# Attention over 16 blocks of heads: K of a block in one load, part of its tokens moved by GpSimd, scores in six pieces

## The chip, the cores and the metric

The kernel runs on one core of one Trainium2 chip. The metric is device time in microseconds (us) of one execution; a difference of about 0.2% is what a measurement of this kernel can tell from none. The engines are TensorE (PE; its weight loads are PEld), VectorE (DVE), ScalarE (ACT), GpSimd (POOL) and SyncE (SP). SP issues every DMA of this kernel, so all transfers run in one queue, in the order in which SP issues them.

## The reference

```python
B, H, Sq, Skv, Dh = 8, 16, 16, 2048, 256      # bfloat16
scores = jnp.einsum('bhqd,bhkd->bhqk', q, k) * Dh ** -0.5
attn = softmax(scores, axis=-1)
return jnp.einsum('bhqk,bhkd->bhqd', attn, v)
```

There are 128 heads, each with 16 queries and 2048 keys of 256 elements. K and V are 134 MB each and every byte of them is read once.

## The kernel before, in words

Eight heads make a block: their 8 x 16 queries are the 128 rows of a score tile. There are G = 16 blocks, numbered 0 to 15 (`last` is 15). A block's K is 8 MB and its V is 8 MB, 128 tokens on each of 128 partitions; below, K(j) and V(j) are those of block j.

**Buffers.** `SL` holds four slots of 64 tokens per partition (4 MB each): VA and VB together are the window of V (`VW`), KA and KB take the two halves of a block's K (half e = 0 or 1 is four heads, loaded in rows of 64 tokens, 32 KB). V comes in rows of 128 tokens, 64 KB. `QT` holds the transposed queries, `O_all` the output of all blocks, `PTz` the transposed probabilities spread over zeros, `QW` the queries of one block spread over zeros.

**Loops.** Each engine runs its own loop over blocks, and semaphores tie them together:

- DVE transposes K in place, 32 tokens at a time (`kt`, L198-200, counted by `c_kt`, and by `c_k0` for block 0), takes the row maximum of the scores (L222), transposes the probabilities twice (L226, L227) and copies a part of them into `PTz` (`copies`, L202).
- PE computes the scores of a block in four groups of 16 matmuls of 512 columns (`qk`, L302), counted by `c_qk`; then `SPARE` = 5 times four matmuls into `X_ps` that nothing reads; then 128 matmuls of probabilities by V (`pv`, L309-320, called PV below), counted by `c_pv` in eight steps a block.
- ACT spreads the next queries into `QW` (`qwb`), takes the exponential (L281-282), makes the rest of the copies (L269) and scales the output (`evac`).
- SP issues K in two halves as soon as the scores of that half of the block before are done (`c_qk`), and V as soon as PV of the block before is done (`c_pv`).
- GpSimd works at the start only: it clears buffers and makes 16 copies of the queries (L184), one behind the other, then clears the second half of `PTz` (L189). The last counts `c_pool` to 2.

**The start.** The queries land in `PTz`, DVE transposes them (L194), and GpSimd copies them from there to `QT`. K(0) is loaded into the slots of V, and K(1) into KA and KB at once behind it, without a wait (L135-137). DVE transposes K(0) as it lands, and then the first half of K(1); only behind that it waits for `c_pool` (L219) and enters its loop. V(0) follows when the scores of the first half of block 0 are done (L140).

**The end.** V of the last two blocks comes in smaller pieces (`PIECES`), and SP issues each when the tokens in its place have been used.

Of the kernel before, what the change touches and what calls it, by code (L numbers as in the profile page):

```python
# [10 lines left out]
SP = mybir.EngineType.SP  # L11
BF16 = mybir.dt.bfloat16
# [3 lines left out]
SPARE = 5  # L16
VA, VB, KA, KB = 0, 1, 2, 3
# [3 lines left out]
def bass_standalone__softmax_full_bidir__sampling_kernel(  # L21
# [16 lines left out]
    ku = k.rearrange("b h s d -> (b h s) d").rearrange("(u p t) d -> u p t d", p=128, t=T)  # L38
# [4 lines left out]
    with ExitStack() as es:  # L43
        ec = es.enter_context
        SL = ec(nc.sbuf_tensor("SL", [128, 4, T, D], BF16))
        QT = ec(nc.sbuf_tensor("QT", [128, SQ * D], BF16))
        QW = ec(nc.sbuf_tensor("QW", [128, 2, 128, 8], BF16))

# [8 lines left out]
        O_all = ec(nc.sbuf_tensor("O_all", [128, G + 2, D], BF16))  # L57
# [8 lines left out]
        def sem(name):  # L66
# [3 lines left out]
        s_k0 = [sem("s_k0a"), sem("s_k0b")]  # L70
        s_k = [sem("s_ka"), sem("s_kb")]
        s_kl = [sem("s_kla"), sem("s_klb")]
        s_v = sem("s_v")
        s_v0 = sem("s_v0")
# [5 lines left out]
        c_k0 = sem("c_k0")  # L80
        c_kt = [sem("c_kt0"), sem("c_kt1")]
# [10 lines left out]

        SLf = SL[:].bitcast(F32)

        QX = PTz[:, 1, 0:SQ * D // 128, :].rearrange("p t m -> p (t m)")

        QXu = QX.rearrange("p (c u a y) -> p a u c y", u=8, a=4, y=2)

        QTu = QT[:].rearrange("p (c u y) -> p u c y", u=32, y=2)

        SLk = SL[:].rearrange("p s (c t) (b i q) -> p s c b q t i", t=16, i=32, q=2)


        PIECES = {last - 1: [(0, 60), (60, 39), (99, 29)],
                  last: [(0, 28), (28, 32), (60, 23), (83, 16), (99, 11), (110, 8), (118, 5), (123, 5)]}

        s_p = {a: sem("s_p%d" % a) for a in sorted({a for w in PIECES for a, n in PIECES[w][1:]})}
        VW = SL[:, VA:VB + 1, :, :].rearrange("p a t d -> p (a t) d")

# [10 lines left out]
        def qx(Q, a):  # L120

            return (QTu[32 * a:32 * a + 32, 8 * Q:8 * Q + 8, :, :].rearrange("p u c y -> p c u y"),
                    QXu[32 * Q:32 * Q + 32, a, :, :, :].rearrange("p u c y -> p c u y"))

        def load_k(eng, g, e, slot, t0, n, s):
            eng.dma_start(SL[:, slot, t0:t0 + n, :], ku[2 * g + e, :, t0:t0 + n, :]).then_inc(s, 16)  # L126

        def on_sync(eng):
            def load_v(w, a, n):

                eng.wait_ge(c_pv, 8 * w + (a + n + C - 1) // C)
                eng.dma_start(VW[:, a:a + n, :], vb[w, :, a:a + n, :]).then_inc(s_p[a] if a else s_v, 16)  # L132

            eng.dma_start(QX, qh).then_inc(s_q, 16)
            for g, s0, s in ((0, VA, s_k0), (1, KA, s_k)):  # L135
                for e in range(2):
                    load_k(eng, g, e, s0 + e, 0, T, s[e])

            for e in range(2):
                eng.wait_ge(c_qk, 4 * e + 4)  # L140
                eng.dma_start(VW[:, T * e:T * e + T, :], vb[0, :, T * e:T * e + T, :]).then_inc(s_v0 if e else s_v, 16)
            for e in range(2):
                eng.wait_ge(c_qk, 4 * e + 12)
                load_k(eng, 2, e, KA + e, 0, T, s_k[e])
            for e in range(2):
                eng.wait_ge(c_pv, 4 * e + 12)
                eng.dma_start(VW[:, T * e:T * e + T, :], vb[1, :, T * e:T * e + T, :]).then_inc(s_v0 if e else s_v, 16)
            with nc.Fori(3, last, engines=[SP], hint_back_edge=True) as j:
                for e in range(2):
                    eng.wait_ge(c_qk, 8 * j + 4 * e - 4)  # L150
                    load_k(eng, j, e, KA + e, 0, T, s_k[e])
                load_v(j - 1, 0, 2 * T)
            for e in range(2):
                eng.wait_ge(c_qk, 8 * last + 4 * e - 4)
                load_k(eng, last, e, KA + e, 0, T // 2, s_k[e])
                load_k(eng, last, e, KA + e, T // 2, T // 2, s_kl[e])
            for w in PIECES:
                for a, n in PIECES[w]:
                    load_v(w, a, n)
            eng.wait_ge(c_ev, G)  # L160
            eng.dma_start(oh[:, 0:last, :], O_all[:, 2:G + 1, :]).then_inc(s_st, 16)
            eng.wait_ge(c_ev, G + 1)
            eng.dma_start(oh[:, last, :], O_all[:, G + 1, :]).then_inc(s_st, 16)
            eng.wait_ge(s_st, 32)

        def on_gpsimd(eng):

            for x, n in ([(c_pv, 8)] + [(x, 1) for x in s_kl] +
                         [(s_p[a], 16 * G - 16 * sum(a in dict(PIECES[w]) for w in PIECES)) for a in s_p]):
                eng.sem_inc(x, n)  # L170
            eng.memset(QW[:].rearrange("p e m x -> p (e m x)").bitcast(F32), 0.0).then_inc(c_qt, 1)
            zero = [PTz[:, e].rearrange("p t c -> p (t c)").bitcast(F32) for e in range(2)]
            eng.memset(zero[0], 0.0).then_inc(c_pool, 1)
            eng.memset(mk[:], 1.0).then_inc(c_mk, 1)
            eng.memset(P_sb[:, 0:16], 0.0).then_inc(c_mk, 1)
            eng.memset(P_sb[:, 2064:2080], 0.0).then_inc(c_mk, 1)
            eng.wait_ge(c_mk, 3)
# [3 lines left out]
            for n in range(16):  # L181

                eng.wait_ge(c_cq if n else c_pool, max(n, 1))
                eng.tensor_copy(*qx(n // 4, n % 4)).then_inc(c_cq, 1)  # L184

            eng.wait_ge(c_qw, 4)
            eng.wait_ge(c_cq, 16)
            eng.wait_ge(c_mk, 7)
            eng.memset(zero[1], 0.0).then_inc(c_pool, 1)  # L189

        def on_vector(eng):
# [6 lines left out]
            def kt(e, h, slot, n=1, first=False):  # L198
                x = SLf[:, slot, 32 * h:32 * h + 32 * n, :].rearrange("p t i -> p (t i)")
                eng.transpose(x, x).then_inc(c_k0 if first else c_kt[e], n)  # L200
# [11 lines left out]
            for e in range(2):  # L212
                eng.wait_ge(s_k0[e], 16)
                for h in range(2):
                    kt(e, h, VA + e, 1, True)

            eng.wait_ge(s_k[0], 16)
            kt(0, 0, KA, 2)
            eng.wait_ge(c_pool, 2)  # L219
            with nc.Fori(0, G, engines=[DVE]) as g:  # L220
                eng.wait_ge(c_qk, 8 * g + 8)
                eng.tensor_reduce(out=negm[:], in_=S_ps[:].rearrange("p c n -> p (c n)"),  # L222
                                  axis=AX.X, op=ALU.max, negate=True).then_inc(c_mx, 1)
                eng.wait_ge(c_ex, g + 1)
                eng.wait_ge(c_co[1], 8 * g + 1)
                eng.transpose(fa[:, 0:2048], P_sb[:, 16:2064]).then_inc(c_pt, 1)  # L226
                eng.transpose(fb[:, 0:2080], P_sb[:, 0:2080]).then_inc(c_pt, 1)  # L227
                eng.reciprocal(rinv[:, bass.ds(g + 2, 1)], lsum[:]).then_inc(c_ri, 1)
                mid = eng.to_reg((g + 15) & 15)
                with eng.If_lt(mid, 14):  # L230
                    eng.wait_ge(s_k[0], 16 * g + 16)
                    kt(0, 0, KA)
# [59 lines left out]
        def on_tensor(eng):  # L292
# [16 lines left out]
            def pv(rr, two):  # L309

                for t in range(2 * T):
# [3 lines left out]
                    if t in s_p:  # L315
                        eng.wait_ge(s_p[t], rr)
# [79 lines left out]
```

## Time and profile before

| | |
|---|---|
| device time, median of 3 runs | 631.43 us (631.23 to 631.60) |
| span of the profiled execution, first to last instruction | 630.1 us |
| what lies outside that span (median less span) | 1.3 us |
| read from HBM, written to it | 269.48 MB, 1.05 MB |
| mean rate over the span | 429 GB/s |
| mean granted TensorE clock | 0.976 |

The page gives no time for the profiled execution beside its span, so the span stands for it, and 1.3 us are added to come to the median. In the lines of the profile a group stands as "line engine operation out<-in shapes xcount | busy us, mean ns of one | idle before, and what ended it"; a row of the timeline as "start us, us, engine line operation out<-in shapes xcount [idle before <- what ended it]"; a piece of the chain as "start us, us, what". "PEq", "SPq" and "DVEq" are an engine's instructions that only issue or wait. A stretch (`a:b`) has the busy time of each engine, then the granted clock, the busy share of the 16 DMA engines and GB/s.

### The profile page before, as it was taken

The numbers are of one execution on the slowest core, as the hardware profiler recorded it, in microseconds if no ns is written. First come the engines' busy times: TensorE is split into PE (matmuls) and PEld (weight loads), VectorE is DVE, ScalarE is ACT, GpSimd is POOL, SyncE is SP. The second block draws the span as 40 slices with busy tenths as digits, with TensorE's granted clock in tenths as the row PEclk, the third lists the DMA queues.
The fourth block names the chain that finished last, engine by engine and source line by source line (L and its number), as shares of the span: only waits on it lengthen the run. The fifth ranks groups of instructions, "written<-read, shape, count | busy, mean of one in ns | idle before, by whom it ended". The sixth has DMA issues, their size and how long they took to land.

```text
span 630.1 us, 7710 instructions
## 1 busy us (share of the span) xinstructions
PE 535.6 (85%) x3336; PEld 273.4 (43%) x2561; DVE 419.4 (67%) x193; ACT 269.1 (43%) x308; POOL 26.0 (4%) x30
## 2 busy tenths in 40 slices
PE   1658989889888898888978889888889878899997
PEld 0112734518244272542726336263362724518386
DVE  1989694865849657496574956749566594768740
ACT  1016562723437243362534525335263352732653
POOL 7800000000000000000000000000000000000000
PEclk9998989999899998999999899999998999999999
DMA  9999999999999999999999999999999999999999
GB/s 377 433 435 431 433 431 424 433 439 426 466 399 466 408 433 441 424 441 424 437 453 408 458 408 458 416 424 441 424 441 449 408 458 408 458 404 421 435 428 376
DMA packets 11008, 270.54 MB, mean 429 GB/s; under 512 B 1024, under 2 KB 3072, under 8 KB 3584
## 3 DMA queue, kind: packets, MB, share of 16 engines
q1 hardware_dynamic: 11008, 270.54, 99.9%
HBM read 269.48 MB, written 1.05 MB: 429 GB/s over the span
## 4 chain that ended last, share of the span: by engine, by line
DMA 57%; PE 34%; issue 4%; DVE 4%; SPq 0%; DVEq 0%; ACT 0%
DMA SL<-in_v_dram 52%; PE O_ps L317 30%; DMA SL<-in_k_dram 5%; DVE SL L200 2%; PE S_ps L296 1%; PE S_ps L297 1%; DVE PTb L227 1%; DVE negm L222 1%; PE X_ps L297 1%; SPq L132 0%; DVE PTz L207 0%; DVE PTz L209 0%; SPq L126 0%; ACT P_sb L282 0%; DVE O_all L247 0%
## 5 line engine op out<-in xcount | busy, mean ns | idle before, releaser
L200 DVE STREAM_TRANSPOSE SL<-SL 128x4096 f32<-128x4096 f32 (+1 forms) x63 | 280.6, 4492 | 88.1 <-DMA SL<-in_k_dram 87.6
L296 PE MATMUL S_ps<-SL,QW 128*128 128x512 bf16 (+1 forms) x512 | 206.1, 403 | 57.6 <-DVE SL L200 48.9
L317 PEld LDWEIGHTS O_ps<-SL,PTz 128*128 128x128 bf16 x2048 | 198.9, 98 | 114.2 <-issue 89.0
L317 PE MATMUL O_ps<-SL,PTz 128*128 128x256 bf16 x2048 | 226.6, 273 | 24.9 <-DMA SL<-in_v_dram 23.8
L297 PE MATMUL S_ps<-SL,QW 128*128 128x512 bf16 (+1 forms) x512 | 205.6, 401 | 0.0
L296 PEld LDWEIGHTS S_ps<-SL,QW 128*128 128x128 bf16 (+1 forms) x512 | 74.4, 145 | 230.1 <-issue 161.9
L256 ACT ACTIVATE QW<-QT 32x256 bf16 x64 | 26.9, 420 | 168.5 <-PE S_ps L297 167.3
L269 ACT ACTIVATE PTz<-PTa 16x1024 bf16<-16x1024 bf16 x32 | 33.8, 1056 | 128.9 <-PE O_ps L317 114.2
L222 DVE TENSOR_REDUCE negm<-S_ps 128x1 f32<-128x2048 f32 x16 | 36.6, 2289 | 58.3 <-PE S_ps L297 58.3
L269 ACT ACTIVATE PTz<-PTa,mk 32x1024 bf16<-32x1024 bf16 x64 | 72.3, 1130 | 0.0
L269 ACT ACTIVATE PTz<-PTb 16x1024 bf16<-16x1024 bf16 x64 | 67.2, 1051 | 1.2
L226 DVE STREAM_TRANSPOSE PTa<-P_sb 128x2048 bf16<-128x2048 bf16 x16 | 37.0, 2312 | 35.4 <-ACT P_sb L282 35.4
L297 PE MATMUL X_ps<-QT,QW 128*128 128x512 bf16 x260 | 58.2, 379 | 0.0
L227 DVE STREAM_TRANSPOSE PTb<-P_sb 128x2080 bf16<-128x2080 bf16 x16 | 36.8, 2302 | 0.0
L269 ACT ACTIVATE PTz<-PTb,mk 32x1024 bf16<-32x1024 bf16 x32 | 36.2, 1132 | 0.0
L282 ACT ACTIVATE P_sb<-S_ps,negm 128x2048 bf16<-128x2048 f32 x16 | 31.5, 1967 | 5.9 <-DVE negm L222 5.9
L262 ACT ACTIVATE O_all<-O_ps,rinv 128x256 f32 x15 | 7.1, 473 | 39.8 <-PE O_ps L317 39.8
L184 POOL COPY QT<-PTz 32x1024 bf16<-32x1024 bf16 x16 | 17.4, 1087 | 2.4 <-DVE PTz L194 1.5
L207 DVE TENSOR_SCALAR PTz<-PTb,mk 32x1024 bf16<-32x1024 bf16 x32 | 15.2, 476 | 0.0
L209 DVE COPY PTz<-PTa 16x1024 bf16<-16x1024 bf16 x32 | 13.5, 422 | 1.1
L247 DVE TENSOR_SCALAR O_all<-O_ps,rinv 128x256 bf16<-128x256 f32 x1 | 0.5, 484 | 20.4 <-PE O_ps L317 20.4
L296 PE MATMUL S_ps<-PTz 128*128 128x512 bf16 x1 | 0.6, 608 | 9.9 <-ACT QW L256 9.9
(18 smaller groups left out, 21.0 us busy)
## 6 DMA issues: line engine op xcount, KB each, us to landing
SL<-in_k_dram SPq DMA_DIRECT2D x30, 4096.0 KB, 24.2
SL<-in_v_dram SPq DMA_DIRECT2D x4, 4096.0 KB, 21.3
SL<-in_k_dram SPq DMA_DIRECT2D x4, 2048.0 KB, 21.5
SL<-in_v_dram SPq DMA_DIRECT2D x1, 3840.0 KB, 21.3
SL<-in_v_dram SPq DMA_DIRECT2D x1, 2496.0 KB, 22.0
SL<-in_v_dram SPq DMA_DIRECT2D x1, 2048.0 KB, 12.2
SL<-in_v_dram SPq DMA_DIRECT2D x1, 1856.0 KB, 24.7
SL<-in_v_dram SPq DMA_DIRECT2D x1, 1792.0 KB, 10.8
```

The lines of the kernel that those rows point to most:

```text
L184: eng.tensor_copy(*qx(n // 4, n % 4)).then_inc(c_cq, 1)
L200: eng.transpose(x, x).then_inc(c_k0 if first else c_kt[e], n)
L207: ins = eng.tensor_scalar(out=dst, in0=src, scalar1=m, scalar2=None, op0=ALU.mult)
L222: eng.tensor_reduce(out=negm[:], in_=S_ps[:].rearrange("p c n -> p (c n)"), axis=AX.X, op=ALU.max, negate=True).then_inc(c_mx, 1)
L226: eng.transpose(fa[:, 0:2048], P_sb[:, 16:2064]).then_inc(c_pt, 1)
L227: eng.transpose(fb[:, 0:2080], P_sb[:, 0:2080]).then_inc(c_pt, 1)
L256: eng.activation(dv, src(a), ACTF.Copy, scale=scale).then_inc(c_qw, 1)
L269: eng.activation(dst, src, ACTF.Copy, scale=m if x else 1.0).then_inc(c_co[e], 1)
L282: eng.activation(P_sb[:, 16:2064], sv, ACTF.Exp, bias=negm[:], scale=1.0, accum_out=lsum[:]).then_inc(c_ex, 1)
L296: return eng.matmul(dst, w, x, start=start, stop=stop, skip_group_check=not check)
L297: return eng.add_instruction(mybir.InstMatmult(name=nc.get_next_instruction_name(), engine=PE, start_tensor_calc=start, stop_tensor_calc=stop,
L317: ins = eng.matmul(O_ps[:, 0:D], PTz[:, t // T, t % T, :], VW[:, t, :], start=(t == 0), stop=(t == 2 * T - 1))
```

## The change

K of a block now comes in one DMA of 64 KB rows into the upper half of `SL` (`KW`, 128 tokens per partition). Behind it lie 47 further tokens (`KX`, `MV` = 47). GpSimd copies the first 47 tokens of `KW` to `KX`, in one instruction per block, for blocks 1 to 14; so K is used from token 47 of the slot to the end of `KX`, and the slot can be loaded again when the copy is done and the scores of the other 81 tokens are (three of six pieces, `CUT`). For blocks 0 and 15 DVE transposes the 47 tokens straight from `KW` into `KX`.

- The scores of a block are made in six pieces of 32, 32, 17, 15, 16 and 16 tokens, with a weight load before each matmul; `SPARE` goes from 5 to 3 and comes ahead of the scores, when the block's K has landed. The halves e are now two sets of 16 partitions of each 32, not two sets of heads in time.
- V stays in one DMA a block; PV reads it from token 47 on, round the end.
- Query and output share one buffer (`OQ`); `QT` and `O_all` are gone.
- DVE takes over four copies a block from ACT; ACT spreads the queries after the exponential, not before it.
- K(0) is loaded into `KW` in four parts. K(1) goes into the same place, part by part, behind scores of block 0 (`c_qk` 1, 2, 3, and `c_kt` 6). V(0) needs no scores any more, and SP issues it behind K(1). DVE's wait for `c_pool` 2 stands ahead of its one loop, which now holds the transposes of K(0) too.

On DVE, at the program's start, before: the transposes of K(0) and of half of K(1) (`s_k0a`, `s_k0b`, `s_ka` are landings of K), then the wait for GpSimd.

```order
L200 STREAM_TRANSPOSE SL<-SL 128x4096 [waits s_k0a]
L200 STREAM_TRANSPOSE SL<-SL 128x4096
L200 STREAM_TRANSPOSE SL<-SL 128x4096 [waits s_k0b]
L200 STREAM_TRANSPOSE SL<-SL 128x4096
L200 STREAM_TRANSPOSE SL<-SL 128x8192 [waits s_ka]
L220 UNCONDITIONAL_BRANCH [waits c_pool]
L220 ISA
L222 TENSOR_REDUCE negm<-S_ps 128x1 [waits c_qk]
```

On DVE, now: the wait for `c_pool`, then the loop. Its first part, up to the second branch of L237, is jumped over in the first round.

```order
L234 UNCONDITIONAL_BRANCH [waits c_pool]
L237 COMPARE_AND_BRANCH
L238 REGISTER_ALU
L239 TENSOR_REDUCE negm<-S_ps 128x1 [waits c_qk]
L242 REGISTER_ALU [waits c_ex]
L242 REGISTER_ALU
L242 ISA
L243 STREAM_TRANSPOSE PTa<-P_sb 128x2048 [waits c_co1]
L244 STREAM_TRANSPOSE PTb<-P_sb 128x2080
L245 ISA
L245 RECIPROCAL rinv<-lsum 128x1
L237 UNCONDITIONAL_BRANCH
```

The rows that follow these in the same loop on DVE: the six transposes of a block's K, the last three behind GpSimd's copy (`c_x`).

```order
L246 COMPARE_AND_BRANCH
L247 ISA
L248 REGISTER_ALU
L250 ISA
L220 STREAM_TRANSPOSE SL<-SL 128x4096 [waits s_k]
L220 STREAM_TRANSPOSE SL<-SL 128x4096 [waits s_kb]
L220 STREAM_TRANSPOSE SL<-SL 128x2176 [waits s_kc]
L258 REGISTER_ALU x2
L259 COMPARE_AND_BRANCH
L220 STREAM_TRANSPOSE SL<-SL 128x1920 [waits c_x]
L220 STREAM_TRANSPOSE SL<-SL 128x2048 x2
```

The transposes of K(0) stood ahead of the wait for `c_pool` and now stand behind it; the transposes of later blocks stand in one run, ahead of the copies.

On SP, at the start, before: queries, K(0) and K(1) without a wait, then V(0) behind scores.

```order
L134 DMA PTz<-in_q_dram 128x4096 [waits barrier_Pool_Activation_PE_DVE_SP_release]
L126 DMA SL<-in_k_dram 128x16384 x4
L141 DMA SL<-in_v_dram 128x16384 [waits c_qk] x2
L126 DMA SL<-in_k_dram 128x16384 [waits c_qk] x2
L147 DMA SL<-in_v_dram 128x16384 [waits c_pv] x2
```

On SP, at the same place, now.

```order
L144 DMA PTz<-in_q_dram 128x4096 [waits barrier_Pool_Activation_PE_DVE_SP_release]
L131 DMA SL<-in_k_dram 128x8192 x2
L131 DMA SL<-in_k_dram 128x4352
L131 DMA SL<-in_k_dram 128x12032
L131 DMA SL<-in_k_dram 128x8192 [waits c_qk] x2
L131 DMA SL<-in_k_dram 128x4352 [waits c_qk]
L131 DMA SL<-in_k_dram 128x12032 [waits c_kt]
L138 DMA SL<-in_v_dram 128x32768 [waits c_pv]
```

K(1) has gained waits for block 0, and V(0) stands behind K(1).

The core of the diff, engine by engine. The sizes and buffers:

```diff
-SPARE = 5
+MV = 47
+CUT = [(0, 32), (32, 32), (64, 17), (81, 15), (96, 16), (112, 16)]
+SPARE = 3
...
-        SL = ec(nc.sbuf_tensor("SL", [128, 4, T, D], BF16))
-        QT = ec(nc.sbuf_tensor("QT", [128, SQ * D], BF16))
+        SL = ec(nc.sbuf_tensor("SL", [128, 4 * T + MV, D], BF16))
...
+        VW, KW, KX = SL[:, 0:2 * T, :], SL[:, 2 * T:4 * T, :], SL[:, 4 * T:4 * T + MV, :]
+        KS = split(SL[:, 2 * T + MV:4 * T + MV, :])
```

SP:

```diff
+            parts = list(zip((MV, MV + 32, MV + 64, 0), (32, 32, 17, MV), (s_k, s_kb, s_kc, s_kx)))
...
+            load_k4(0, [])
+            load_k4(1, [(c_qk, 1), (c_qk, 2), (c_qk, 3), (c_kt, 6)])
+            load_v(0, 0, 2 * T)
+            with nc.Fori(2, last - 1, engines=[SP], hint_back_edge=True) as j:
+                eng.wait_ge(c_qk, 6 * j - 3)
+                eng.wait_ge(c_x, j)
+                load_k(eng, j, KW, 0, 2 * T, s_k)
                 load_v(j - 1, 0, 2 * T)
```

GpSimd:

```diff
-                eng.wait_ge(c_cq if n else c_pool, max(n, 1))
-                eng.tensor_copy(*qx(n // 4, n % 4)).then_inc(c_cq, 1)
+            for n, (x, m) in enumerate(firsts):
...
+                eng.wait_ge(*prev)
+                eng.tensor_copy(*qx(n // 4, n % 4)).then_inc(x, 1 if x is c_cq else m)
+                prev = (x, m)
...
             eng.memset(zero[1], 0.0).then_inc(c_pool, 1)
+            with nc.Fori(1, last, engines=[POOL]) as n:
+                eng.wait_ge(c_qk, 6 * n)
+                eng.wait_ge(s_k, 16 * n + 16)
+                eng.wait_ge(s_kx, ((n + 2) & 16) + 32)
+                eng.sem_inc(c_mk, 1)
+                eng.tensor_copy(KX.rearrange("p t d -> p (t d)"),
+                                KW[:, 0:MV, :].rearrange("p t d -> p (t d)")).then_inc(c_x, 1)
```

DVE, the start and the middle of the loop:

```diff
-            for e in range(2):
-                eng.wait_ge(s_k0[e], 16)
-                for h in range(2):
-                    kt(e, h, VA + e, 1, True)
-            eng.wait_ge(s_k[0], 16)
-            kt(0, 0, KA, 2)
             eng.wait_ge(c_pool, 2)
-            with nc.Fori(0, G, engines=[DVE]) as g:
+            with nc.Fori(0, G + 1, engines=[DVE]) as h:
...
+                    eng.wait_ge(s_k, h16)
+                    kt(0, KA, KA)
+                    eng.wait_ge(s_kb, w)
+                    kt(1, KA, KA)
+                    eng.wait_ge(s_kc, w)
+                    kt(2, KA, KA)
+                    mid = eng.to_reg(g)
+                    with eng.If_lt(mid, last - 1):
+                        eng.wait_ge(c_x, h + 1)
+                        for i in (3, 4, 5):
+                            kt(i, KX, KX)
...
+                    copies(0, (2, 3))
+                    eng.wait_ge(c_pv, 8 * h)
+                    copies(1, (2, 3))
```

PE:

```diff
+            def qk(dst, x):
+                for e in range(2):
+                    for bp in range(8):
+                        ins = mm(dst, QW[:, e, bp, :], x[:, :, bp // 2, 16 * e:16 * e + 16, bp % 2],
+                                 e + bp == 0, e == 1 and bp == 7, True)
                 return ins
...
+                    with eng.If_lt(mid, last - 1):
                         with nc.Fori(0, SPARE, engines=[PE]) as x:
+                            eng.wait_ge(s_k, 16 * r + 16)
+                            spare()
+                    for i, (t, n) in enumerate(CUT):
+                        eng.wait_ge(c_kt, 6 * r + i + 1)
+                        c, m = t // 32, t % 32
+                        qk(S_ps[:, c, 16 * m:16 * m + 16 * n], KS[:, t:t + n]).then_inc(c_qk, 1)
```

More of the change, by code (lines that the diff above doesn't have):

```diff
@@ L11 @@
 SP = mybir.EngineType.SP
+POOL = mybir.EngineType.Pool
 BF16 = mybir.dt.bfloat16
@@ L157, in on_sync @@
+            eng.wait_ge(c_qk, 6 * last - 9)
+            eng.wait_ge(c_x, last - 1)
+            load_k2(last - 1)
+            load_v(last - 2, 0, 2 * T)
+            eng.wait_ge(c_qk, 6 * last - 3)
+            eng.wait_ge(c_x, last)
+            load_k4(last, [])
             for w in PIECES:
@@ L289, in on_scalar @@
                     evac(g + 1)
[L290 removed]
+                copies(1, (0, 1))
         def on_tensor(eng):
```

238 lines of the change are left out of this document (104 added, 134 removed).

## The prediction

> **What bounds the kernel now.** I read the busy shares on the page first, then stretches of the loop and of the start, then the chain of waits.
>
> ```profile
> PE 535.6 (85%) x3336; PEld 273.4 (43%) x2561; DVE 419.4 (67%) x193; ACT 269.1 (43%) x308; POOL 26.0 (4%) x30
> DMA  9999999999999999999999999999999999999999
> q1 hardware_dynamic: 11008, 270.54, 99.9%
> ```
>
> No engine is busy throughout, but the one DMA queue is: 99.9% of 16 engines' span. Four stretches, two at the start and two of one block each, say how fast it runs (the last two figures are the DMA share and GB/s):
>
> ```profile
> 15.00:25.00 10.00, 4.68 (x11) 0.94 (x6) 8.77 (x2) 0.00 (x0) 9.51 (x9) 1.00 0.99 429
> 25.00:41.00 16.00, 12.55 (x48) 3.32 (x23) 14.82 (x3) 0.00 (x0) 4.93 (x3) 1.00 0.99 428
> 274.86:313.64 38.78, 33.31 (x214) 17.08 (x161) 26.06 (x13) 16.66 (x20) 0.00 (x0) 1.00 1.00 433
> 313.64:352.42 38.78, 33.29 (x214) 17.06 (x161) 26.06 (x13) 16.67 (x20) 0.00 (x0) 1.00 1.00 433
> ```
>
> The start is as full as the loop. The chain of waits gives the loop's rhythm, and the timeline of DVE the moment at which half a K has landed:
>
> ```profile
> 272.56 24.24 DMA SL<-in_v_dram
> 296.80 0.23 issue
> 297.03 14.15 PE O_ps L317 x128
> ...
> 311.34 24.24 DMA SL<-in_v_dram
> 335.58 0.23 issue
> 306.54 4.45 DVE L200 STREAM_TRANSPOSE SL<-SL 128x4096 f32<-128x4096 f32 x1 [6.58 <-DMA SL<-in_k_dram]
> ```
>
> A V lands every 335.58 - 296.80 = 38.78 us, in which 16.78 MB move. V is issued 24.24 us before it lands, though it needs about half of 38.78, so it stands some 4.8 us behind K in the queue: the chain by V and PV is closed, but the queue is what sets the time. Two rules for the sum follow. A transfer that needs less engine time gives its saving; any moment in which the queue stands empty is added in full, since nothing later runs below the full rate and could catch up.
>
> **The rows of 64 KB.** The first half of K lands at about 306.54, 9.7 us behind the V at 296.80; two halves are 19.4, and what is left of 38.78 for V, in 64 KB rows, is 19.4 too. The two differ by what these times resolve: 0.0 to 0.1 us a block. Twelve blocks (2 to 13) get one load: 0 to 1.2 us gained; a loss is excluded, since V's rows of 64 KB already run at the full rate, and I take 0.7, near the middle. The parts of K(0) and K(1) cost under 0.1.
>
> The Trainium skill, DMA: Bandwidth & Descriptors, Anatomy of one DMA, fits a transfer as about 2.0 us fixed and its bytes at 436 GB/s. By that, twelve loads fewer would be 24 us less. The trace disagrees for a full queue: 4.19 MB in 9.7 us is 432 GB/s with nothing fixed left over.
>
> **The start.** Now the wait of DVE for `c_pool` stands ahead of the transposes of K(0). Behind it on DVE is everything, and behind that, by semaphores, the first scores on PE, K(1) on SP (part one waits for the first piece of scores), and V(0), which could go at once but stands behind K(1) on SP. So I walk from GpSimd to SP. The rows of GpSimd, its groups, and those of DVE and PE at the start:
>
> ```profile
> 8.16 18.32 POOL L184 COPY QT<-PTz 32x1024 bf16<-32x1024 bf16 x16 [1.52 <-DVE PTz L194]
> 26.59 3.52 POOL L189 MEMSET PTz<- 128x4096 f32 x1
> L184 POOL COPY QT<-PTz 32x1024 bf16<-32x1024 bf16 x16 | 17.4, 1087 | 2.4 <-DVE PTz L194 1.5
> L171 POOL MEMSET QW<- 128x1024 f32 x1 | 1.0, 951 | 1.1 <-POOLq L381 1.1
> L179 POOL MEMSET mk<- 16x1 f32 x4 | 0.4, 91 | 0.2
> 15.46 8.77 DVE L200 STREAM_TRANSPOSE SL<-SL 128x4096 f32<-128x4096 f32 x2 [7.36 <-DMA SL<-in_k_dram]
> 25.17 8.77 DVE L200 STREAM_TRANSPOSE SL<-SL 128x4096 f32<-128x4096 f32 x2 [0.94 <-DMA SL<-in_k_dram]
> 20.32 0.65 PE L296 MATMUL S_ps<-SL,QW 128*128 x1 [8.49 <-DVE SL L200]
> 25.03 0.57 PE L297 MATMUL S_ps<-SL,QW 128*128 x1
> 25.44 0.38 PE L296 MATMUL S_ps<-SL,QW 128*128 x1
> 25.66 0.38 PE L297 MATMUL S_ps<-SL,QW 128*128 x1
> ```
>
> - GpSimd starts its copies at 8.16 as before. Twelve of them keep 1024 elements, at 18.32 / 16 = 1.145 us with the gap; four have 768. With 91 ns for an instruction that does almost nothing, 768 elements cost 0.09 + 0.75 x 1.00 + 0.06 = 0.90. Sum 12 x 1.145 + 4 x 0.90 = 17.3, end 25.5; the clear of 3.52 behind it ends at 29.1. Bounds: 30.1 if nothing is shorter; 25.9 if the copies ran at the clear's rate (3.52 / 4096 = 0.86 ns an element, 0.66 and 0.88 us a copy and 0.06 of gap each).
> - The first transpose, 32 tokens: 4.4, to 33.5.
> - PE begins 0.4 later (before: 20.32, with the first of the two transposes done at 19.9). Its first matmuls came every 0.43 us, eleven of them up to 25.03, and then every 0.22. Sixteen: 11 x 0.43 + 5 x 0.22 = 5.8, and 0.2 for the end: 39.9. Bounds 3.5 (all at 0.22) and 6.9 (all at 0.43).
> - SP issues part one of K(1). From issue to landing, beside the transfer itself, two rows give bounds:
>
> ```profile
> PTz<-in_q_dram SPq DMA_DIRECT2D x1, 1024.0 KB, 5.0
> out_dram<-O_all SPq DMA_DIRECT2D x1, 64.0 KB, 1.6
> ```
>
>   5.0 less 2.4 (1.05 MB at 433 GB/s) is 2.6 for the very first DMA; 1.6 less 0.2 is 1.4 for the last. I take 1.4, since the queue has run before.
> - K(0) lands complete at 25.2, as before (the same bytes behind the same queries). From there the queue is empty until K(1): 39.9 + 1.4 - 25.2 = **16.1 us**. Bounds: 25.9 + 4.4 + 0.1 + 3.5 + 0.2 + 1.4 - 25.2 = 10.3, and 30.1 + 4.4 + 0.5 + 6.9 + 0.2 + 2.6 - 25.2 = 19.5.
>
> What is late next? Part two waits for the second piece: transposed at 37.9, scored by 39.9 + 16 x 0.22 = 43.4, while part one takes until 46. Part three and four (all transposes done by about 47.5) and V(0) come sooner than the queue needs them. So it stays full from 41 on.
>
> **The loop.** K(j) lands at 0; V(j-1) fills the queue until 19.4 and K(j+1) until 38.8. Two issues must come in time: K(j+1) before 19.4 - 1.4 = 18.0 and V(j) before 37.4.
>
> - GpSimd's copy, 47 x 256 = 12,032 elements, has no row. By the short copies, (1087 - 91) / 1024 = 0.97 ns an element, it is 11.8 us; in proportion to 1087 it is 12.8; at the clear's rate 10.3. I take 11.8.
> - DVE: three transposes (81 tokens at 4.4 per 32) to 11.2, then the wait for the copy (`c_x`, 11.9), behind which stand three transposes, 6.5 long, to 18.4, and four copies:
>
> ```profile
> L207 DVE TENSOR_SCALAR PTz<-PTb,mk 32x1024 bf16<-32x1024 bf16 x32 | 15.2, 476 | 0.0
> L209 DVE COPY PTz<-PTa 16x1024 bf16<-16x1024 bf16 x32 | 13.5, 422 | 1.1
> ```
>
>   2 x 0.48 + 2 x 0.42 = 1.8, to 20.2. PE's last piece (16 matmuls of 256 columns, 14.15 / 128 = 0.11 each) ends at 20.4.
> - K(j+1): twelve spare matmuls take 12 x 0.43 = 5.1 at most, so pieces one to three end at about 8.6, 12.4 and 14.7. Issue 14.7, needed by 18.0.
> - V(j): PV(j-1) runs from 20.6 for 14.15 us. Issue 34.9, needed by 37.4.
>
> So the loop stays full, with the queue as its cover. It holds until the copy takes 11.8 + 2.5 = 14.3 us; each us beyond costs one in each of 14 blocks. The extra waits (SP's for `c_x`, with V behind it; PE's for K ahead of the spares) lie within these times. The four copies that ACT loses and the queries that it spreads later are off this path. The last V is cut as before in its last pieces, so I count the end at nothing.
>
> The Trainium skill, GPSIMD Engine Reference, Elementwise — side-by-side cycle accounting, has 1.03 cycles an element for the simplest bodies and about 1.8 at best for a tight loop, at 1.2 GHz: as an estimate from that page, 10.3 or 18.0 us. The short copies' 0.97 ns (1.17 cycles) lie near the first; by the second the loop would not stay full, which is the first rival.
>
> **Sum.** 630.1 + 16.1 - 0.7 + 0.1 (parts) = 645.6, and 1.3 for what lies outside the span: 646.9, taken as **647.0 us**, 2.5% slower.
>
> **Rivals.**
>
> 1. *The long copy is slower than the short ones.* The only row for GpSimd reading SBUF has 32 partitions and 1024 elements; the long one has 128 and 12,032. From 14.3 us on, V(j) is late. At 1.5 times its rate, 17.7 us, 14 x 3.4 = 48 us come on top: 695. For it: no row of this size. Against it: the clears of 128 partitions keep 0.84 ns an element beyond the first 91 ns, at 1024 (951 ns) as at 4096 (3520 ns). Chance 0.10.
> 2. *Not slower: the start stays covered.* If GpSimd's preamble ended so early that the first piece is scored by 25.2 - 1.4 = 23.8, K(1) would follow K(0) without a gap, and what remains is 631.4 - 0.6 = 630.8. That needs `c_pool` at about 13.3, so copies and clear in 5.1 us, where the clear alone takes 3.5 and one copy 1.1. Chance 0.03.
> 3. *Loads have a fixed cost that the fuller queue hides.* Then twelve loads fewer give 12 x 1.4 = 17 more (the 1.4 of the 64 KB store): about 630.0 with the gap at the start, and it needs that gap to be short to come out clearly faster. The share of 1.00 in the loop speaks against it. It is the rule of the Trainium skill's page named above, as a mechanism of this kernel. Chance 0.02.
>
> **How the numbers follow.** The forecast has 0.85. Its bounds: 630.1 + 10.3 - 1.2 + 1.3 = 640.5 and 630.1 + 19.5 - 0 + 0.1 + 1.3 = 651.0. They leave out only the rivals, 0.15, so they are the range. About 0.2% (1.3 us) is what a measurement of this kernel can tell from no change. Slower: the forecast and rival 1, 0.95. Within 0.2%: rival 2, 0.03. Faster: rival 3, 0.02.
>
> **What would show it.** In the changed profile: one slice of the DMA row near zero behind 25 us, about 16 us of the queue empty; DVE's first transpose of K at about 29, released by GpSimd's last clear; the loop still 38.7 to 38.8 from V to V at 433 GB/s; a GpSimd copy of 10.3 to 12.8 us; transposes four to six waiting under 1 us for it. A first transpose at about 10, as the first part of K(0) lands, would make the start wrong; a period above 38.8 with the queue empty between K and V would make the loop wrong, and the copy's row would say whether rival 1 is the reason.

## The result, and the profile after

The changed kernel takes 649.16 us (median of 5 runs, 648.62 to 651.16) where the kernel before takes 631.25 (631.23 to 631.60): a ratio of 1.0286, 95% interval 1.0274 to 1.0299. Forecast were 647.0 us and a range of 640.5 to 651.0. The profiled execution (span 649.8) is the slowest of the five; the other four have spans of 647.1 to 647.8, so at least 2 us of its span are its own.

From the page of the kernel after, the busy shares, the DMA rows and the queues:

```profile
PE 526.1 (81%) x3752; PEld 346.2 (53%) x3584; DVE 446.0 (69%) x290; ACT 257.6 (40%) x240; POOL 167.2 (26%) x43
DMA  9549999999999999999999999999999999999998
GB/s 365 216 198 445 452 448 391 444 424 428 440 407 444 440 424 428 448 420 424 452 444 399 448 452 420 420 452 444 403 444 452 420 420 434 457 401 427 431 425 330
q1 hardware_dynamic: 9568, 270.54, 97.1%
q8 instruction: 2, 0.03, 0.0%
```

The same bytes move. The load is lost in the second and third slice (16.2 to 48.7 us), and from there on the DMA row is full. Two packets of a queue called "instruction", 16,384 bytes each, are new: one at 50.14, among the parts of K(1), and one at 647.77, beside the last store. That store lands 2.85 us after its issue, where in e1 below, whose trace has no second packet, it takes 1.70; that the one makes the other is not shown. Stretches of the kernel after: three at the start, then two of one block each, from V to V (the last two figures are the DMA share and GB/s):

```profile
15.00:25.00 10.00, 0.00 (x0) 0.00 (x0) 0.00 (x0) 0.00 (x0) 9.40 (x10) 1.00 0.94 405
25.00:41.00 16.00, 7.29 (x23) 2.77 (x24) 11.80 (x4) 0.00 (x0) 3.35 (x1) 1.00 0.05 11
41.00:48.00 7.00, 7.00 (x56) 5.15 (x55) 5.75 (x3) 0.00 (x0) 0.00 (x0) 1.00 0.91 386
276.59:315.28 38.69, 33.62 (x238) 21.62 (x224) 27.66 (x19) 16.03 (x15) 10.21 (x1) 0.91 1.00 434
315.28:353.98 38.70, 33.22 (x238) 21.49 (x224) 27.70 (x19) 16.04 (x15) 10.21 (x1) 0.91 1.00 434
```

The stretch from 25 to 41 had a DMA share of 0.99 before and has 0.05 now. From 15 to 25 only GpSimd and the queue work, and DVE and PE wait; behind 25 the queue waits too. A block of the loop takes 38.70 us instead of 38.78. The timeline of the kernel after, with GpSimd's end of the preamble, DVE's transposes of K(0), SP's issue of K(1) and V(0), and the first copy:

```profile
8.12 16.60 POOL L196 COPY OQ<-PTz 32x768 bf16<-32x768 bf16 x16 [2.29 <-issue]
24.83 3.52 POOL L202 MEMSET PTz<- 128x4096 f32 x1
29.20 17.54 DVE L220 STREAM_TRANSPOSE SL<-SL 128x4096 f32<-128x4096 f32 x6 [21.22 <-POOL PTz L202]
39.80 7.30 SPq L131 DMA_DIRECT2D SL<-in_k_dram  x4
47.15 0.43 SPq L138 DMA_DIRECT2D SL<-in_v_dram  x1
63.20 10.21 POOL L208 COPY SL<-SL 128x12032 bf16<-128x12032 bf16 x1 [34.85 <-DMA SL<-in_k_dram]
```

This is the walk of the prediction: the clear ends at 28.35, and DVE begins at 29.20 after 21.22 us of waiting for it, though the first part of K(0) landed at 10.54. SP issues K(1) at 39.80. By the landing times in the trace, K(1) is complete at 63.05; before it was at 44.57. These 18.5 us make the result: the last piece of V lands 18.0 later than before (645.18, was 627.21).

The loop in the kernel after, GpSimd's copies (each starts 0.36 us after a K has landed) and SP's issues:

```profile
257.56 10.21 POOL L208 COPY SL<-SL 128x12032 bf16<-128x12032 bf16 x1 [28.50 <-DMA SL<-in_k_dram]
271.74 0.33 SPq L131 DMA_DIRECT2D SL<-in_k_dram  x1
291.42 0.33 SPq L138 DMA_DIRECT2D SL<-in_v_dram  x1
296.29 10.21 POOL L208 COPY SL<-SL 128x12032 bf16<-128x12032 bf16 x1 [28.51 <-DMA SL<-in_k_dram]
310.47 0.33 SPq L131 DMA_DIRECT2D SL<-in_k_dram  x1
334.98 10.21 POOL L208 COPY SL<-SL 128x12032 bf16<-128x12032 bf16 x1 [28.48 <-DMA SL<-in_k_dram]
```

K lands at 295.93, V at 315.28, the next K at 334.62. K is issued at 310.47, 4.8 us ahead of the landing of the V in front of it, and V at 291.42, 4.5 us ahead of the K in front of it. Call this the lead of a load: the time from its issue to the landing of the load in front. It decides the later experiments. A load whose lead is long enough lands 19.35 us behind the one in front; what it takes beyond that is called late below.

### The profile page after: what moved, and what is told of

It is laid out like the page before. It is cut to its first block, busy times and chain, and to the rows that moved or that the text cites. A ratio compares the mean times of both kernels' runs of the same rounds, so it can differ in the third digit from the quotient of the medians.

```text
span 649.8 us, 9361 instructions
## 1 busy us (share of the span) xinstructions
PE 526.1 (81%) x3752; PEld 346.2 (53%) x3584; DVE 446.0 (69%) x290; ACT 257.6 (40%) x240; POOL 167.2 (26%) x43
## 4 chain that ended last, share of the span: by engine, by line
DMA 49%; PE 24%; DVE 11%; issue 8%; POOL 2%; ACT 1%; DVEq 0%; SPq 0%; ACTq 0%; POOLq 0%
DMA SL<-in_k_dram 49%; PE S_ps L327 18%; DVE SL L220 9%; PE X_ps L328 4%; PE O_ps L351 2%; POOL SL L208 2%; DVE negm L239 1%; ACT QW L285 1%; DVE PTb L244 1%; POOL PTz L202 1%; ACT PTz L299 0%; DVE PTz L229 0%; DVE PTz L227 0%; SPq L131 0%; ACT P_sb L310 0%
## 5 line engine op out<-in xcount | busy, mean ns | idle before, releaser
L220 DVE STREAM_TRANSPOSE SL<-SL 128x4096 f32<-128x4096 f32 (+2 forms) x96 | 280.9, 2988 | 134.7 <-DMA SL<-in_k_dram 104.2
L327 PEld LDWEIGHTS S_ps<-SL,QW 128*128 128x128 bf16 x1536 | 147.0, 98 | 265.9 <-DVE SL L220 170.6
L327 PE MATMUL S_ps<-SL,QW 128*128 128x512 bf16 (+3 forms) x1536 | 235.6, 312 | 46.4 <-DVE SL L220 46.1
L208 POOL COPY SL<-SL 128x12032 bf16<-128x12032 bf16 x14 | 143.0, 10213 | 406.0 <-DMA SL<-in_k_dram 406.0
L328 PE MATMUL X_ps<-P_sb,QW 128*128 128x512 bf16 x168 | 66.5, 577 | 66.8 <-DMA SL<-in_k_dram 56.7
L285 ACT ACTIVATE QW<-OQ 32x256 bf16 x60 | 80.2, 1337 | 1.1
L299 ACT ACTIVATE PTz<-PTa,mk 32x1024 bf16<-32x1024 bf16 x32 | 36.2, 1131 | 0.0
L299 ACT ACTIVATE PTz<-PTb 16x1024 bf16<-16x1024 bf16 x32 | 33.5, 1047 | 0.4
L196 POOL COPY OQ<-PTz 32x1024 bf16<-32x1024 bf16 (+1 forms) x16 | 15.7, 980 | 3.2 <-issue 2.3
L227 DVE TENSOR_SCALAR PTz<-PTa,mk 32x1024 bf16<-32x1024 bf16 x32 | 15.2, 476 | 0.0
```

Of the source, the lines that this page charges most:

```text
L208: eng.tensor_copy(KX.rearrange("p t d -> p (t d)"), KW[:, 0:MV, :].rearrange("p t d -> p (t d)")).then_inc(c_x, 1)
L220: eng.transpose(words(dst[:, t % 81:t % 81 + n, :]), words(src[:, t % 81:t % 81 + n, :])).then_inc(c_kt, 1)
L227: ins = eng.tensor_scalar(out=dst, in0=src, scalar1=m, scalar2=None, op0=ALU.mult)
L285: eng.activation(dv, src(a).rearrange("p e (q b) y -> p e q b y", b=4), ACTF.Copy, scale=scale).then_inc(c_qw, 1)
L299: eng.activation(dst, src, ACTF.Copy, scale=m if x else 1.0).then_inc(c_co[e], 1)
L327: return eng.matmul(dst, w, x, start=start, stop=stop, skip_group_check=not check)
```

## The experiments

The theory: the whole loss is the gap at the start, and the gap is DVE's one wait for the preamble. The rivals: the loop pays (the copy, the later issues), or the new order of the loads does. The kernel before, measured along with each run, took 631.3 us.

### The wait behind block 0 (e1)

```diff
-            eng.wait_ge(c_pool, 2)               # DVE, ahead of its loop
             with nc.Fori(0, G + 1, engines=[DVE]) as h:
...
                 with eng.If_ne(hh, 0):
+                    eng.wait_ge(c_pool, 2)
                     eng.wait_ge(c_qk, 6 * h)
```

> The changed kernel, with DVE's wait for GpSimd's preamble moved from ahead of the transposes of K(0) into the part of the loop that the first round jumps over. Theory (the wait alone empties the queue): the first transpose starts when 2 MB of K(0) have landed, at about 10.6 us instead of 29.2; the first piece is scored at about 21, K(1) is issued before K(0) has landed at 25.2, and the 18.4 us by which K(1) was late go: 649.2 - 18.4 = 630.8 us, within 1 us. The loop keeps its 38.70 us. Rival (one slot for K is the cause: K(1) behind scores of K(0) can't follow in time whatever DVE waits for): a gap of several us stays between K(0) and K(1), 635 to 645 us.

Measured: 632.75 us (11 runs, 632.10 to 633.31), a ratio of 1.0020 [1.0011, 1.0029] to the kernel before. Its timeline:

```profile
10.48 4.45 DVE L220 STREAM_TRANSPOSE SL<-SL 128x4096 f32<-128x4096 f32 x1 [2.59 <-DMA SL<-in_k_dram]
20.79 11.30 SPq L131 DMA_DIRECT2D SL<-in_k_dram  x4
24.74 3.52 POOL L202 MEMSET PTz<- 128x4096 f32 x1
46.47 10.21 POOL L208 COPY SL<-SL 128x12032 bf16<-128x12032 bf16 x1 [18.21 <-DMA SL<-in_k_dram]
```

DVE begins with the first part of K(0), K(1) is issued 19 us earlier, and K(1) is complete at 46.31. GpSimd's preamble is as long as ever and costs nothing. One moved wait returns 16.4 us of 17.9: the gap is shown to be that wait. The granted clock of TensorE, 0.976 before and 0.932 in the changed kernel, is 0.935 here, so the lower clock is not what the 16.4 us were lost to. But 1.4 us more than before are left, 2 above the expected 630.8.

### The same wait put into the kernel before (e2)

```diff
+            eng.wait_ge(c_pool, 2)               # DVE, ahead of the first transposes of K(0)
...
-            eng.wait_ge(c_pool, 2)               # DVE, behind them
```

> The kernel before, with only the wait for GpSimd's preamble moved ahead of the transposes of K(0). K(1) has slots of its own there and is in the queue until 44.6 us. Theory (the wait costs what the queue can't cover): V(0) is issued at about 44.5 instead of 31.5, with some 2 us of gap, and K(2) some 10 us later than before, with about 4 us of gap: 4 to 10 us, 635 to 641 us. Rival (the wait costs its own lateness, whatever else is queued): 18 us as in the changed kernel, 649 us.

Measured: 643.10 us (2 runs), 1.0185 [1.0167, 1.0204]: 11.8 us longer, and more than the 4 to 10 that I expected. DVE's first transposes, two stretches, and SP's issues of K(2):

```profile
29.69 26.02 DVE L200 STREAM_TRANSPOSE SL<-SL 128x4096 f32<-128x4096 f32 x5 [21.80 <-POOL PTz L189]
40.00:60.00 20.00, 13.45 (x51) 3.46 (x24) 18.00 (x4) 2.01 (x5) 0.00 (x0) 0.99 0.78 311
60.00:75.00 15.00, 11.79 (x43) 3.28 (x22) 13.02 (x9) 10.13 (x11) 0.00 (x0) 0.78 0.77 315
71.38 9.76 SPq L126 DMA_DIRECT2D SL<-in_k_dram  x2
```

DVE waits as long as in the changed kernel, but two blocks of K are in flight, so the queue runs dry later and in three places. It is empty for 0.22 x 20 + 0.23 x 15 = 7.9 us; the cost is 11.8. By the landing times, the three loads behind a stop land 3.6, 2.1 and 4.4 us late (against 9.71 for such a load in a full queue), 10.1 together: a stop loses some 0.7 us more than the queue stands empty. The rest is the second half of K(2): issued at 80.81, 2.8 us before the half in front of it lands, it lands 1.6 us late, though the queue is not empty there.

### V(0) ahead of K(1) (e3)

```diff
-            load_k4(1, [(c_qk, 1), (c_qk, 2), (c_qk, 3), (c_kt, 6)])
             load_v(0, 0, 2 * T)
+            load_k4(1, [(c_qk, 1), (c_qk, 2), (c_qk, 3), (c_kt, 6)])
```

> The changed kernel, with V(0) issued ahead of K(1) and all waits kept. Theory (with one slot for K and one for V the queue has nothing else to fetch): no gap behind K(0), since V(0) takes the queue from 25.2 to 44.6, but K(1) lands at 64 us instead of 63, GpSimd's copy of it ends at 74 and K(2) is issued at 75, some 13 us after the queue ran empty; V(1) may add 2 to 3 us: 644 to 650 us. Rival (only the order on SP is wrong): the 18.4 us go, 631 us.

Measured: 650.20 us (2 runs, 648.72 and 651.69), 1.0298. Two stretches:

```profile
25.20:41.00 15.80, 7.41 (x25) 2.89 (x26) 11.91 (x4) 0.00 (x0) 3.04 (x1) 1.00 0.92 398
60.00:75.00 15.00, 14.14 (x60) 4.70 (x48) 10.19 (x3) 8.03 (x8) 9.37 (x1) 0.82 0.19 80
```

V(0), which waits for nothing, fills the old gap, and the same gap opens one load later (0.81 x 15 = 12.2 us of it in this stretch): V(1) and K(2) hang on block 1's scores, and these on K(1). Another load in front hides no wait that the next block's work has.

### A longer copy (e4, e9)

```diff
                 eng.wait_ge(s_kx, ((n + 2) & 16) + 32)
+                eng.sem_inc(c_mk, 1)
+                eng.tensor_copy(KX[:, 0:24, :]..., KW[:, 0:24, :]...).then_inc(c_cq, 1)     # e9: 18
+                eng.wait_ge(c_cq, n + 7)
                 eng.sem_inc(c_mk, 1)
                 eng.tensor_copy(KX..., KW[:, 0:MV, :]...).then_inc(c_x, 1)
```

The extra copy of 24 (e4) or 18 (e9) tokens runs ahead of the full one, and only the full one counts `c_x`.

> The changed kernel, with 24 of the 47 tokens copied twice by GpSimd, so that the copy takes about 15.6 us instead of 10.2. Theory (the loop is covered up to a copy of 13.2 to 14.7 us, and pays 1 us a block beyond): V(j) becomes late by 1 to 2.4 us in 13 blocks, the period goes from 38.7 to 39.7 to 41.1 us: 662 to 681 us. Rival (the copy matters only for the issue of K, which is needed 18 us after the landing): 649 us, period 38.7.

> The changed kernel with 18 of the 47 tokens copied a second time by GpSimd behind the first copy (nothing else computed differently): copies of 10.2 and, by 18 x 256 elements at 0.85 ns, 3.9 us, with some 0.3 between and behind them, so 4.2 us longer than in the changed kernel. The prediction had the loop covered up to a copy of 14.3 us in all, by which this one is hidden: 649.2. The run with 24 tokens copied twice was 5.5 us longer and cost 2.2 to 2.4 us a block, so that the cover is 3.2 us (a copy of 13.4): by that, 4.2 costs 1.0 in each of 14 blocks, 663. If no cover is there and the cost begins elsewhere: 649.2 + 14 x 4.2 = 708.

Measured: 682.52 us (e4, 2 runs) and 669.84 (e9, one run). The timeline of e9, GpSimd and SP:

```profile
343.87 4.03 POOL L208 COPY SL<-SL 128x4608 bf16<-128x4608 bf16 x1 [26.05 <-DMA SL<-in_k_dram]
348.06 10.21 POOL L212 COPY SL<-SL 128x12032 bf16<-128x12032 bf16 x1 [0.16 <-POOL SL L208]
358.49 0.33 SPq L131 DMA_DIRECT2D SL<-in_k_dram  x1
381.30 0.33 SPq L138 DMA_DIRECT2D SL<-in_v_dram  x1
382.57 4.03 POOL L208 COPY SL<-SL 128x4608 bf16<-128x4608 bf16 x1 [24.29 <-DMA SL<-in_k_dram]
422.70 4.03 POOL L208 COPY SL<-SL 128x4608 bf16<-128x4608 bf16 x1 [25.72 <-DMA SL<-in_k_dram]
```

Both copies take 14.40 us, and V is issued 381.30 - 343.51 = 37.8 after K has landed. By the prediction (cover up to 14.3, V needed by 37.4) that costs 0.1 to 0.4 a block; it costs 20.7 / 14 = 1.5. e4, 15.7 us of copies, costs 33.4 / 14 = 2.4. So the prediction's price of the cover is wrong by about 1 us a block. Nor is it the straight line that e4 alone suggested (no cost up to 13.4, 663 for e9). In e9 V has a lead of 0.9 us at 381.30 and lands 1.4 late, and two loads on, with 2.0, it lands 2.4 late; K with 4.4 to 6.8 lands in time or up to 0.5 late.

### K's rows at 32 KB (e6)

```diff
-                load_k(eng, j, KW, 0, 2 * T, s_k)
+                load_k(eng, j, KW, T, T, s_k)
+                load_k(eng, j, KW, 0, T, s_k)
```

(On top of e1. The waits that count this semaphore go with it, and the first part of K of blocks 14 and 15 is cut in two so that the counts agree.)

> The kernel of e1, with each K of blocks 2 to 13 loaded in two DMAs of 64 tokens (32 KB rows) into the same places, issued together (and the first parts of K of blocks 14 and 15 cut in two, so that the counts agree). Theory (the shorter period of the loop, 38.70 against 38.78 us, is the rows of 64 KB): the period goes back to 38.77 to 38.80, 632.75 + 1.0 = 633.4 to 634.0 us. Rival (the period is shorter for another reason, such as fewer issues or later V): 632.7 us, period 38.70.

Measured: 633.61 us (6 runs), 0.86 over e1. Copies of e6, then of e1:

```profile
279.43 10.22 POOL L214 COPY SL<-SL 128x12032 bf16<-128x12032 bf16 x1 [28.53 <-DMA SL<-in_k_dram]
318.22 10.22 POOL L214 COPY SL<-SL 128x12032 bf16<-128x12032 bf16 x1 [28.57 <-DMA SL<-in_k_dram]
```

```profile
279.17 10.21 POOL L208 COPY SL<-SL 128x12032 bf16<-128x12032 bf16 x1 [28.49 <-DMA SL<-in_k_dram]
317.88 10.21 POOL L208 COPY SL<-SL 128x12032 bf16<-128x12032 bf16 x1 [28.49 <-DMA SL<-in_k_dram]
```

From K to K 38.79 against 38.71: one load in 64 KB rows is worth 0.08 us a block, 0.96 in twelve, against two in 32 KB rows. Forecast were 0.7. The 0.86 alone is less than the 0.2% that a measurement can tell; the period in the traces decides it.

### The left-over 1.4 us (e5, e7, e8)

In the records of the packets, e1 has one 16,384-byte packet of the instruction queue at 33.39, beside K(1), and the part of K(1) that lands next lands 6.4 us behind the one before, where the same part of K(0) takes 4.9. One of the 16 DMA engines is from then on 1.5 us behind the others, and every load waits for it. The kernel before has neither the packet nor the late part. K(1) is complete 1.7 us later than before (46.31, was 44.57); the shorter period of the loop takes 0.9 of it back by the last V (628.09, was 627.21). The other 0.5 us are lost at the end. The chain of the kernel before, then that of e1:

```profile
612.16 15.05 DMA SL<-in_v_dram
627.26 0.73 PE O_ps L317 x5
```

```profile
615.09 14.15 PE O_ps L351 x128
```

Before, the last V sets the end. In e1 PV of block 15 does: it starts behind ACT's scaling of block 14 and runs to 629.24, 1.1 us past the landing of the last V.

Three edits on top of e1:

e5 takes PE's scores of block 0 out of its loop:

```diff
+            ...                              # the scores of block 0, then:
-            with nc.Fori(0, G + 1, engines=[PE], hint_back_edge=True) as r:
+            with nc.Fori(1, G + 1, engines=[PE], hint_back_edge=True) as r:
```

> The kernel of e1, with PE's scores of block 0 written ahead of its loop, so that PE doesn't jump over the code of PV in its first round. In the traces of the changed kernel and of e1, a 16 KB packet of a queue for instructions (q8) runs for 0.97 us on one of the 16 DMA engines just as PE ends the scores of block 0 (50.1 and 33.4 us), and the part of K(1) then in flight lands 1.4 and 1.6 us late, by that one engine. Theory (PE's jump makes it fetch code through that engine, and as the queue never runs empty the loss stays to the end): no such packet before the last microseconds, K(1) complete at 44.7 instead of 46.3, 632.75 - 1.55 = 631.2 us. Rival (the lateness is that of the smaller parts of K(0) and K(1)): 632.7 us, the parts of K(1) late as in e1.

e7, on top of e5, moves four of DVE's copies:

```diff
                     eng.tensor_reduce(out=negm[:], ...).then_inc(c_mx, 1)
...
+                        copies(1, (2, 3))        # of the block before, in the wait for the exponential
                     eng.wait_ge(c_ex, h)
...
-                    copies(1, (2, 3))            # at the end of the trip
```

> The kernel of e5, with the four copies that DVE took over from ACT moved from ahead of the next row maximum to behind it, where DVE waits 2.4 us for the exponential in each block. At the end of e1, PV of block 15 starts 1.7 us after PV of block 14 ends, because the probabilities come late, and the last store is issued 2.9 us after the last V, against 1.3 us before. Theory (DVE's order makes PV(15) late, and with it the end): PV(15) starts about 1 us earlier, the last V sets the end again, 631.2 - 0.5 = 630.7 us, just faster than the kernel before. Rival (the end is set by the queue and the store of the first 15 blocks): as e5, 631.2 us.

e8 gives PE's loop one empty trip at the very start, which jumps over scores and PV:

```diff
-            with nc.Fori(0, G + 1, engines=[PE], hint_back_edge=True) as r:
+            with nc.Fori(0, G + 2, engines=[PE], hint_back_edge=True) as z:
...
+                r = (z + 31) & 31                # 31 in the first trip: neither scores nor PV
```

> e1 (the changed kernel with the wait for GpSimd's preamble behind the loop's start) with one empty trip of TensorE's loop ahead of the sixteen: it jumps over the scores and over PV before the first load has landed. In e1 and the runs built on it, one packet of 16,384 bytes of a queue called instruction lies among the loads (at 33.39 in e1, 33.72 with the 32 KB rows, 35.67 and 35.55 with the first scores peeled), and the load that lands next lands 1.3 to 1.6 us late, on one of the 16 DMA engines, for good; before has neither. Theory: the packet is code that TensorE meets for the first time behind the scores; the empty trip fetches it while the queries land, and K(1) then lands complete near 44.8 instead of 46.3: 631.2, e1 less 1.5. Rival 1: the packet comes with every first jump over PV behind the scores, whatever was run earlier, or belongs to another engine: it stays near 33, 632.7. Rival 2: the packet goes, but the late landing has another cause: K(1) still lands near 46.2 and the time stays 632.7.

Measured: 632.72 (e5), 633.27 (e7), 632.68 us (e8); e1 has 632.75. None is faster. But the packet moves with PE's program: to 35.67 in e5 and 35.55 in e7, and to 5.81 in e8. The queues of e8 between 4 and 7 us, and its timeline:

```profile
q1 hardware_dynamic: 121, 1.31, 103.6%
q8 instruction: 1, 0.02, 1.9%
```

```profile
11.99 4.45 DVE L220 STREAM_TRANSPOSE SL<-SL 128x4096 f32<-128x4096 f32 x1 [3.97 <-DMA SL<-in_k_dram]
46.38 10.21 POOL L208 COPY SL<-SL 128x12032 bf16<-128x12032 bf16 x1 [17.99 <-DMA SL<-in_k_dram]
```

Now the first part of K(0) is the late one (DVE starts at 11.99, in e1 at 10.48), all parts behind it come at their usual distance, and K(1) is complete at 46.23 as in e1. The load behind the packet is the late one in each of the five kernels (the changed one, e1, e5, e7 and e8), so the packet is shown to be the cause of the late landing, and PE's program its owner. What the time would be without it, these runs don't show: in them the packet only moved. It takes one engine for 0.93 to 1.07 us, and in a queue that is never empty this is added wherever it falls. The Trainium skill, Runtime: NRT & Kernel Launch, Instruction fetch mechanics, says that each engine's program comes in blocks of 16 KiB through a DMA queue of its own sequencer, at a cost that is mostly hidden. The size and the owner agree; that it is hidden does not hold here, where the load behind it lands 1.3 to 1.5 us late.

As for e7, which was aimed at the end: PV of block 15 starts at 614.41, in e5 at 614.59, in both behind ACT's scaling of block 14 and not behind these copies. V's lead is 4.5 us as in e1, and nothing is gained; 0.5 more is within the spread of the runs (632.61 to 634.11).

### Scores in four pieces again (e10)

```diff
-                    for i, (t, n) in enumerate(CUT):
-                        eng.wait_ge(c_kt, 6 * r + i + 1)
+                    for c, (i, x) in enumerate([(1, 1), (2, 1), (4, 2), (6, 2)]):
+                        eng.wait_ge(c_kt, 6 * r + i)
...
+                        qk(S_ps[:, c, :], KS[:, 32 * c:32 * c + 32]).then_inc(c_qk, x)
```

(On top of e1.)

> e1 (the changed kernel with the wait for GpSimd's preamble behind the loop's start) with TensorE's scores in four pieces of 32 tokens, as before, instead of six; DVE's transposes stay in six, and pieces three and four of the scores wait for two transposes each. TensorE's program has 66 instructions less. The run with an empty trip of TensorE's loop showed that the packet of 16,384 bytes among the loads is TensorE's code and comes where it first runs behind the scores. Theory: the shorter program needs no such packet during the loads (the kernel before, with a program of about this length, has none): K(1) lands complete near 44.8 instead of 46.3, and the time is e1's less 1.5, 631.2. Rival: the packet stays, and the time with it, 632.7; or the later issue of V (the last piece of scores ends 1.8 us later, V is issued some 2.8 instead of 4.6 us ahead of the queue's end) costs the loop more than 0.05 us a block, and the time lies above 631.8 though the packet is gone.

Measured: 651.58 us (5 runs, 650.73 to 651.88), 1.0318 [1.0303, 1.0332], 18.8 over e1. The queues, the timeline (GpSimd, SP) and ten blocks from V to V of e10:

```profile
q1 hardware_dynamic: 9568, 270.54, 98.2%
q14 instruction: 1, 0.01, 0.0%
```

```profile
325.26 10.21 POOL L208 COPY SL<-SL 128x12032 bf16<-128x12032 bf16 x1 [28.66 <-DMA SL<-in_k_dram]
341.94 0.33 SPq L131 DMA_DIRECT2D SL<-in_k_dram  x1
366.13 10.21 POOL L208 COPY SL<-SL 128x12032 bf16<-128x12032 bf16 x1 [30.66 <-DMA SL<-in_k_dram]
```

```profile
145.94:547.21 401.27, 332.02 (x2040) 184.03 (x1919) 276.67 (x181) 160.38 (x150) 102.13 (x10) 0.93 0.98 417
```

The same ten blocks of e1:

```profile
143.19:530.39 387.20, 332.06 (x2362) 214.91 (x2240) 276.97 (x181) 160.37 (x150) 102.13 (x10) 0.93 1.00 433
```

The q8 packet is gone (the one of q14 comes behind the last load) with 66 of PE's instructions. But a block takes 40.1 us instead of 38.7: the third piece now waits for tokens that come through GpSimd's copy, so K is issued 17.0 us after the K before has landed, not 14.5. The V in front lands at 344.54, so K has a lead of 2.6 us, and lands 21.2 behind it where 19.35 would do. The six pieces are what buys K its lead, and 2.6 us of lead are not enough here. I expected V's issue to be the sore spot; it was mainly K's: of the 14 us by which these ten blocks are longer, late Ks are 11.7 and late Vs 2.6. The first copy of e10:

```profile
46.39 10.21 POOL L208 COPY SL<-SL 128x12032 bf16<-128x12032 bf16 x1 [18.06 <-DMA SL<-in_k_dram]
```

K(1) is complete at 46.23, as in e1, and not at the expected 44.8, though no packet lies among its parts: its third part is issued at 34.10, with a lead of 1.2 us, and lands 1.2 late. So e10 does not show what a shorter program without the packet is worth.

## Why the prediction was right, and where its steps failed

- **The start (16.1).** Right in its steps: the wait for the preamble, the first transpose (29.2 to 33.7) and K(1)'s issue (forecast 39.9, measured 39.80). Some luck is in this: GpSimd ended at 28.35, 0.75 earlier than forecast, and DVE began 0.85 behind it, where the walk had nothing. The queue stands empty for 0.06 x 10 + 0.95 x 16 + 0.09 x 7 = 16.4 us. e1 shows the cause, e3 that V(0) in front does not cover it. The time to the end of K(1) grew by 18.5, though, and two sums were missing. The restart: part one of K(1) lands at 47.06, 7.26 us after its issue, 2.4 more than the 4.9 of such a part in a full queue, where 1.4 was taken (2.6 was the upper bound). And PE's instruction packet: part two lands 6.2 behind part one instead of 4.9, 1.3 that the prediction had nowhere. The restart and the packet, 1.0 and 1.3, are about the 2.2 us between 647.0 and 649.16.
- **The rows (-0.7).** Right: e6 measures -0.9, by 0.08 us a block.
- **The loop (nothing lost).** Right as a result, since ten blocks take 387.4 us where before they took 387.8. The copy took 10.21, the lower bound (10.3), not 11.8: the large copy runs at the clear's rate (0.85 ns an element), not at the short copies'. At 1.2 GHz that is 1.02 cycles, so of the two figures that the prediction cited from the Trainium skill (GPSIMD Engine Reference, Elementwise — side-by-side cycle accounting) the 1.03 holds. PE and DVE ran as forecast: K issued 14.5 after K has landed (forecast 14.7), V 34.2 (34.9).
- **The step that failed** is "Issue 14.7, needed by 18.0" and "34.9, needed by 37.4", with its cover "until the copy takes 14.3". An issue 1.4 us before the queue runs dry is not in time. The leads of e9, e10, e4, e1 and the kernel after say so together: at 4.4 us or more a load lands at most 0.1 late, with few exceptions up to 0.5; at 3.4 to 3.8, 0.2 to 0.9; at 2.3 to 3.3, anything from nothing to 2.5; at 0.6 to 2.0, 1.4 to 2.4, and once 0.7; issued 0.7 to 1.6 us after the queue's end, 3.3 to 4.1. So the lead that the sum should have asked for is about 4.4 us, not 1.4, and the real cover of the loop was under 1 us, not 2.5. That the forecast of the loop came out is luck: it happens to stand at leads of 4.5 and 4.8, where K's first half had 14.4 before.
- **The end (nothing).** Not quite: from the landing of the last V to the end of the span it is 2.87 us before, 3.38 in e1 and 3.47 in e8, so about 0.5 were lost (4.62 in the profiled execution of the changed kernel). PV of block 15 then ends behind the last V, as e1's chain shows.
- **The rivals.** The copy did not slow, the start did not stay covered (its condition, a preamble that ends by 13.3, is off by 15 us), and no fixed cost of loads came back. (The Trainium skill, DMA: Bandwidth & Descriptors, Anatomy of one DMA, gives the fit of 2.0 us and 436 GB/s that the prediction names for DMAs that GpSimd issues; here SP issues all of them, so the 24 us don't follow from it.) A variant of the second does exist: with the wait moved (e1), 632.75 instead of its 630.8.

What stays open: why loads with a lead of 2 to 3 us are late by such different amounts. In the records some 64 KB packets take up to 4.2 us instead of 2.4: between 150 and 540 us, 161 of 2,497 are above 2.6 in e10, and 25 in e1. That would fit, but no run took those packets apart. No kernel tried beats the one before, and the threshold of PE's program length for the extra packet was only bracketed by e1 and e10.

## What to carry to other kernels

Where one queue sets the time, walk each wait from its engine to the next DMA issue: a preamble on an idle engine is free until somebody waits for it ahead of the first loads' work, and a gap there is added in full. Don't ask whether an issue comes before the queue is dry, but how long before: here 4.5 us were safe, and leads of 2.3 to 3.2 for K, with 3.5 to 5.9 for V, cost 1.4 us a block (e10). Merging loads makes each issue later, so read the lead of the merged load first.

## What the runs showed of the hardware

- Code loading shares the DMA engines. One 16 KB packet of PE's program delays the load behind it by 1.3 to 1.5 us (e1, e5, e7, e8), and later loads wait for that engine.
- The first load into an empty queue lands 2.4 us later after its issue than its transfer in a full queue takes (changed kernel, 7.26 against 4.9). In e2 three stops lose 10.1 us for 7.9 us of emptiness.
- A load issued 1.3 us before the one in front lands is 1.5 us late, with 4.5 us it is in time (e9 and the changed kernel).
- GpSimd copies 12,032 bf16 elements on 128 partitions in 10.21 us while DVE, PE and the DMA queue are busy, and takes the same in all 14 blocks.
- A packet of 64 KB takes 2.42 us on its engine at best; a K of 8.4 MB in one load of such rows saves 0.08 us against two loads in rows of 32 KB (e6).
